# Sliding-window attention and two feed-forward nets on one core: the place of the softmax reciprocals up to step 9, and the first loads

## The chip, the core and the metric

The kernel runs on 1 core of one Trainium2 chip. The metric is the device time of one launch in microseconds (us), the median of three runs. Five engines work side by side, each through its own queue in order: TensorE (PE; its weight loads are listed as PEld), VectorE (DVE), ScalarE (ACT), GpSimd (POOL) and SyncE (SP, which here only issues transfers). They wait for each other through semaphores.

## What is computed

```python
scores = scale * np.matmul(q, k.transpose(0, 1, 3, 2))
keep = (pos[None, :] < n_sink) | ((rel >= 0) & (rel < window))
scores = np.where(keep, scores, -1e9)
a = np.exp(scores - np.max(scores, axis=-1, keepdims=True))
a = a / (np.sum(a, axis=-1, keepdims=True) + 1e-09)
attn_out = np.matmul(a, v)

x = attn_out rearranged to (1536, 512)
x = ((x @ w_a) * (x @ w_b)) @ w_out
h = np.maximum(x @ w_in, 0.0)
out = (h * h) @ w_out2
```

Batch 2, 8 heads, 768 tokens, head dimension 64, 4 sink tokens and a window of 128. The first net is 512 to 1536 to 512, the second 512 to 2048 to 512. All inputs are float32; the sink count and the window come in as data.

## The kernel before

**Groups and steps.** The attention is cut into 24 groups: 2 batches, 6 blocks of 128 queries, and in each block two halves of 4 heads. Group g belongs to block g // 2. The main loop (`attention_fast`) runs steps g = 0, 1, 2, ...; in step g each stage works on the group g plus its lag. The order of the work on PE, DVE, ACT and POOL is written out by hand: a list of (stage, lag) pairs is walked in every step, and each engine gets its instructions in the order of that list (`manual_schedule`). SP's transfers are placed by the scheduler.

```python
ORDER = [
    ("exp0", -1), ("exp1", -1), ("fm", 0), ("pst", -2), ("rec", -1), ("st", -2), ("fu", 0), ("scores0", 0),
    ("x0", -3), ("scores1", 0), ("x1", -3), ("xs", -3), ("abs", 0), ("xh", -3), ("ptp", -2), ("th", -2), ("cast", -2), ("soft0", 0), ("soft1", 0), ("sp", -1),
    ("norm", -1), ("warm", 0), ("fill", 0), ("normA", -1), ("normP", -1), ("xl", -3), ("stt", -1),
    ("lo", -2), ("ts", 0), ("lu", -2), ("stt2", -1)]
AT_FIRST = [x for x in ORDER if x[0] not in ("rec", "warm")]
AT_FIRST.insert(AT_FIRST.index(("soft1", 0)) + 1, ("rec", -1))
AT_FIRST.insert(AT_FIRST.index(("ptp", -2)), ("warm", 0))
```

Steps below `EARLY` (4) use AT_FIRST, all later ones ORDER. The two differ in two places. In ORDER the reciprocals of group g-1 (`rec`) stand on DVE in front of the maxima of group g (`soft0`, `soft1`); in AT_FIRST they stand behind them. In ORDER the warm matmuls stand on PE behind the transposes `ptp`; in AT_FIRST in front of them.

**The stages of one group,** with the lines of the kernel before: `scores0` and `scores1` (L243, PE, into the two PSUM tiles sc); `soft0` and `soft1` (DVE: a predicated copy L259, then two fused add-and-maximum operations L262 each); `exp0` and `exp1` (L270, ACT, four exponentials with their sums); `rec` (L275 and L276, DVE, the reciprocals of the sums); `sp` (L305 to L307, POOL, the sink columns); `norm` (L283, DVE), `normA` (L290, ACT) and `normP` (L295, POOL), which scale the rows of different heads; `pst` (L337, PE, transposes the sink columns) and `st` (L343, ACT, copies them); `ptp` (L313, PE, transposes the probabilities) and `th` (L317, ACT, copies them); `lu` (L328 and L330, POOL, two triangular selections); `x0`/`x1` (L362, from step 10 on L376, PE, times the values) and `xs` (L392, PE, the sink part); `xh` (L400, ACT) and `xl` (L403, DVE), the high and low half of the result.

A buffer rule: `scores0` of group g+1 writes the PSUM tile that `soft0` of group g has read. `pst` of group g-2 stands on PE in front of `scores0` of group g, in both lists.

**Beside the attention.** From step 4 on single pieces of the weights are decoded and split: `abs` (L589) and `cast` (L605) on ACT, `ts`, `stt`, `stt2`, `lo` (L593, L594, L597, L600, L607) on DVE; the pieces begin in steps 4, 8, 10, 11, 12 and so on (`DECODE`). From the end of step 11 on PE gets 12 matmuls of the first net (L720) in each step, `fill`. Below step 10 PE has `warm` instead: matmuls on zeros (L414) whose result nobody reads, as many per step as the table `WARM` says, and 14 before step 0. From step 10 on (`WIDE`) the product with the values is cut in two, `x0` and `x1`, and `x1` waits for a one-element memset on POOL (`mark`, L382) that itself waits for `x0`.

**Sinks.** The sink rows of the values of each batch are split into a high and a low part by `sink_split`: one copy on ACT (L220) and one subtraction on POOL (L221), emitted at the end of the steps in `VS` = (3, 12), the first for batch 0, the second for batch 1.

**Loads.** `load_kq(n)` brings block n's keys (L195) and queries (L196), `load_v(n)` the values (L202), all from SP. The first block comes in two halves. The keys in device memory lie in pieces of 136 floats (128 keys and 8 sink keys), 544 bytes, four pieces to a partition, without a gap. ACT issues only the 2 KB of `raw` (L81) and then loads its function table, placed in front of a one-column exponential (L85).

Of the kernel before, what the change touches and what calls it, by code (L numbers as in the profile page):

```python
# [10 lines left out]
F32 = mybir.dt.float32  # L11
F32R = mybir.dt.float32r
I32 = mybir.dt.int32
U32 = mybir.dt.uint32
AF = mybir.ActivationFunctionType
# [4 lines left out]
P = 128  # L20
# [14 lines left out]
AT_FIRST = [x for x in ORDER if x[0] not in ("rec", "warm")]  # L35
AT_FIRST.insert(AT_FIRST.index(("soft1", 0)) + 1, ("rec", -1))
AT_FIRST.insert(AT_FIRST.index(("ptp", -2)), ("warm", 0))
EARLY = 4
DECODE = [4, 8, 10, 11, 12, 13, 14, 15, 18, 19, 20]
WIDE = 10  # L40
VS = (3, 12)
FLAG = 22
SPARED = range(10, 18)
PINNED = 3
WARM0 = 14
WARM = {0: 2, 1: 4, 2: 6, 3: 8, 4: 9, 5: 6, 6: 6, 7: 6, 8: 6, 9: 6}
NQ, NV, NEX, NTH, NLU, NSP = 3, 5, 3, 2, 2, 2
T = 512
SW = P + SK
HK = P // 2  # L50
PREV = HK + SK
BIG = 8.0e9
# [24 lines left out]
def setup(tc, cp, tp, span):  # L77
    nc = tc.nc
    c = Attn()
    raw = cp.tile([P, 4], I32, name="raw")  # L80
    nc.scalar.dma_start(raw, span.bitcast(I32))  # L81
    ident = tp.tile([P, P], F32, name="ident")
    make_identity(nc, ident)
    warm = tp.tile([P, 1], F32, name="warm")
    nc.scalar.activation(warm, ident[:, 0:1], AF.Exp)  # L85

    v = nc.vector
    d = tp.tile([P, P], F32, name="d")
    nc.gpsimd.iota(d, pattern=[[-1, P]], base=0, channel_multiplier=1, allow_small_or_imprecise_dtypes=True)
    c.col = tp.tile([P, P], F32, name="col")  # L90
    nc.gpsimd.iota(c.col, pattern=[[1, P]], base=0, channel_multiplier=0, allow_small_or_imprecise_dtypes=True)
    c.upf = tp.tile([P, P], F32, name="up")
    v.tensor_scalar(out=c.upf, in0=d, scalar1=0.0, scalar2=None, op0=ALU.is_lt)

    c.rel = tp.tile([P, P], F32, name="rel")
    v.scalar_tensor_tensor(out=c.rel, in0=c.upf, scalar=float(P), in1=d, op0=ALU.mult, op1=ALU.add)
    rel0 = c.spare = tp.tile([P, P], F32, name="rel0")
    v.scalar_tensor_tensor(out=rel0, in0=c.upf, scalar=BIG, in1=d, op0=ALU.mult, op1=ALU.add)
    lo = cp.tile([P, 2], F32, name="lo_f")
    hi = cp.tile([P, 2], F32, name="hi_f")  # L100
    v.tensor_copy(lo, raw.bitcast(U32)[:, 0:4:2])
    v.tensor_copy(hi, raw[:, 1:4:2])
    par = cp.tile([P, 2], F32, name="par")
    v.scalar_tensor_tensor(out=par, in0=hi, scalar=4294967296.0, in1=lo, op0=ALU.mult, op1=ALU.add)
    c.ns = par[:, 0:1]
    c.w = par[:, 1:2]


    m0 = cp.tile([P, P], F32, name="m0")
    m1 = cp.tile([P, SW], F32, name="m1")  # L110
    m2 = cp.tile([P, SW], F32, name="m2")
    c.m = [m0, m1, m2]
    c.sink = tp.tile([P, P], F32, name="sink")
    out_of(v, c.sink, c.col, c.ns)
    out_of(v, m0, rel0, c.w)
    v.tensor_tensor(out=m0, in0=m0, in1=c.sink, op=ALU.max)
    c.identr = cp.tile([P, P], F32R, name="identr")
    v.tensor_copy(c.identr, ident)
    c.ident = c.identr.bitcast(F32)
    return c  # L120


# [34 lines left out]
def attention_fast(tc, ctx, c, cp, tp, q, k, v, vs_in, xh, xl, beside):  # L157


    nc = tc.nc  # L160
# [26 lines left out]
    queries, vals = {}, {}  # L187

    def load_kq(n, part=slice(0, H // 2)):
        if n >= B * NB:  # L190
            return
        if n not in queries:
            queries[n] = p2.tile([P, H // 2, P], F32, name="queries", tag="queries", bufs=NQ)
        b, i = divmod(n, NB)
        nc.sync.dma_start(keys[:, part, i], k[b, i, :, part])  # L195
        nc.sync.dma_start(queries[n][:, part], q[b, i, :, part])  # L196

    def load_v(n):
        if n >= B * NB:
# [4 lines left out]
    with tc.high_priority(offset=1000):  # L204
        load_kq(0, slice(0, 2))
        load_kq(0, slice(2, 4))
    load_kq(1)
    load_v(0)


# [1002 lines left out]
def layout(inputs):  # L1213

    import numpy as np

    def pairs(a, n):

        B, H, S, D = a.shape
        a = a.reshape(B, H // 2, 2, S // n, n, D).transpose(0, 3, 2, 5, 1, 4)  # L1220
        return a.reshape(B, S // n, 2 * D, H // 2, n)

    def blocks(w, inner):

        if inner:
            K, FF = w.shape
            w = w.reshape(K // P, P, FF // P, P).transpose(2, 1, 0, 3)
        return np.ascontiguousarray(w.reshape(-1, P, 512)).view(np.int64)

    q, k, v = (np.asarray(inputs[n]) for n in "qkv")  # L1230
    B, H, S, D = v.shape
    out = {"q": pairs(q, P)}
    sinks = pairs(k[:, :, 0:SK], SK)
    out["k"] = np.concatenate([pairs(k, P), np.broadcast_to(sinks, (B, S // P, *sinks.shape[2:]))], axis=4)
    out["v"] = v.reshape(B, H, S // P, P, D).transpose(0, 2, 3, 1, 4)

    vs = np.zeros((3, 4, SK, B, H // 4, 2, 2, D), v.dtype)
    for j in range(4):
        vs[:, j, :, :, :, j // 2, j % 2] = v[:, j::4, 0:SK].transpose(2, 0, 1, 3)
    out["vs"] = vs.reshape(12 * SK, B, H // 2, 2 * D)  # L1240
    out["span"] = np.broadcast_to(np.stack([inputs["n_sink"], inputs["window"]]).astype(np.int64), (P, 2))
    for n in _INS[5:]:
        out[n] = blocks(np.asarray(inputs[n]), not n.endswith("out"))
    return out
# [16 lines left out]
```

## Time and profile before

| | |
|---|---|
| median of 3 runs | 623.58 us (623.38 to 623.77) |
| profiled execution | 624.48 us |
| its span, first to last instruction | 622.8 us |
| PE busy | 608.0 us (98%) |
| DVE busy | 480.4 us (77%) |
| ACT busy | 303.5 us (49%) |
| POOL busy | 64.8 us (10%) |
| mean granted clock of PE | 0.996 |

The profiled execution took 0.9 us more than the median; 1.7 us of it lie outside the span. The busy shares are averages over stages with different limits: the attention ends at about 110 us, and the change is in its first 60 us. In the rows below a timeline row is: start in us, duration in us, engine, line, operation, what is written from what, shapes, how many were merged, and in brackets the idle time in front of it and who ended it. A PE row with a weight load in front of it is pipelined, so PE rows may overlap.

### The profile page before, as it was taken

Reading aid. Unit: us, or ns where it says so; the run is one execution under the profiler, and the core shown is the slowest. Engines: PE = TensorE matmul, PEld = TensorE weight load, DVE = VectorE, ACT = ScalarE, POOL = GpSimd, SP = SyncE. Lnnn points to the kernel's source line nnn. Section 1 sums busy time; section 2 is a strip of 40 time slices with the busy share of each in tenths; the row PEclk is TensorE's granted clock in tenths of the full one; section 3 lists DMA queues with packets and bytes.
Section 4 is the critical chain, followed back from the end, with each engine's and each line's share of the span. In section 5 each row is a group of like instructions: output and inputs, shape, how many; then the busy total and the mean of one; then the engine's idle time right before and its main releaser. Section 6 shows DMA issues by size and latency. Waiting matters only on the chain.

```text
span 622.8 us, 9656 instructions
## 1 busy us (share of the span) xinstructions
PE 608.0 (98%) x3525; PEld 494.4 (79%) x3525; DVE 480.4 (77%) x1079; ACT 303.5 (49%) x688; POOL 64.8 (10%) x157
## 2 busy tenths in 40 slices
PE   7989999999999999999999999999999999999995
PEld 4667778888888888888888888888888888888884
DVE  6889989369999948858869999977796779834352
ACT  5888887434744434434443554564453445232220
POOL 5665355400000000000000000000000000000000
PEclk9999999999999999999999999999999999999998
DMA  8934423012123313212302013232022202000032
GB/s 260 280 115 148 154 69 103 3 34 73 62 103 115 122 34 102 68 34 68 101 35 101 2 34 102 67 132 82 27 100 67 74 29 68 0 1 0 2 115 94
DMA packets 22041, 49.55 MB, mean 80 GB/s; under 512 B 2080, under 2 KB 8736, under 8 KB 21984
## 3 DMA queue, kind: packets, MB, share of 16 engines
q1 hardware_dynamic: 21696, 48.70, 24.5%
q8 instruction: 30, 0.49, 0.3%
q14 instruction: 27, 0.22, 0.1%
q10 hardware_dynamic: 288, 0.13, 0.1%
HBM read 45.68 MB, written 3.15 MB: 78 GB/s over the span
## 4 chain that ended last, share of the span: by engine, by line


## 5 line engine op out<-in xcount | busy, mean ns | idle before, releaser
L720 PE MATMUL psa<-xh,wh 128*128 128x512 f32 x224 | 88.6, 396 | 0.1
L720 PE MATMUL psa<-xh,wl 128*128 128x512 f32 x224 | 87.4, 390 | 0.0
L720 PE MATMUL psa<-xl,wh 128*128 128x512 f32 x224 | 87.3, 390 | 0.0
L980 PE MATMUL acc<-wh,gh 128*128 128x512 f32 x192 | 74.7, 389 | 0.0
L980 PE MATMUL acc<-wh,gl 128*128 128x512 f32 x192 | 74.7, 389 | 0.0
L980 PE MATMUL acc<-wl,gh 128*128 128x512 f32 x192 | 74.7, 389 | 0.0
L607 DVE TENSOR_TENSOR wl<-wtmp,wh 128x512 fp32r<-128x512 f32 x68 | 48.5, 717 | 17.2 <-ACT wh L605 17.0
L605 ACT CAST wh<-wtmp 128x512 fp32r<-128x512 f32 x68 | 42.3, 622 | 36.8 <-PE acc L980 10.0
L73 ACT CAST gh<-ks 128x512 fp32r<-128x512 f32 x48 | 29.7, 622 | 52.5 <-PE acc L980 52.5
L589 ACT ACTIVATE wtmp<-wraw 128x512 f32<-128x512 f32 x68 | 45.5, 673 | 19.3 <-DVE wl L74 12.7
L980 PE MATMUL acc<-gh,wh 128*128 128x512 f32 x136 | 52.9, 389 | 0.0
L980 PE MATMUL acc<-gl,wh 128*128 128x512 f32 x136 | 52.9, 389 | 0.0
L980 PE MATMUL acc<-gh,wl 128*128 128x512 f32 x136 | 52.9, 389 | 0.0
L720 PEld LDWEIGHTS psa<-xh,wh 128*128 128x128 f32 x224 | 42.1, 188 | 8.9 <-DVE gs L737 0.6
L720 PEld LDWEIGHTS psa<-xh,wl 128*128 128x128 f32 x224 | 42.0, 188 | 8.9
L597 DVE SCALAR_TENSOR_TENSOR wtmp<-wraw,wtmp 128x512 int32<-128x512 int32 x68 | 48.6, 719 | 0.4
L720 PEld LDWEIGHTS psa<-xl,wh 128*128 128x128 f32 x224 | 42.1, 188 | 8.2
L600 DVE SCALAR_TENSOR_TENSOR wtmp<-wraw,wtmp 128x512 int32<-128x512 int32 x68 | 46.4, 687 | 0.7
L980 PEld LDWEIGHTS acc<-wl,gh 128*128 128x128 f32 x192 | 36.0, 188 | 7.5
L980 PEld LDWEIGHTS acc<-wh,gh 128*128 128x128 f32 x192 | 36.0, 188 | 7.4
L980 PEld LDWEIGHTS acc<-wh,gl 128*128 128x128 f32 x192 | 36.0, 188 | 7.4
L74 DVE TENSOR_TENSOR gl<-ks,gh 128x512 fp32r<-128x512 f32 x48 | 32.8, 688 | 10.5 <-ACT gh L73 10.1
(177 smaller groups left out, 1279.5 us busy)
## 6 DMA issues: line engine op xcount, KB each, us to landing
wraw<-in_moe_w_out_dram SPq DMA_DIRECT2D x28, 512.0 KB, 3.5
wraw<-in_moe_w_in_dram SPq DMA_DIRECT2D x16, 512.0 KB, 3.5
wraw<-in_moe_w_a_dram SPq DMA_DIRECT2D x12, 512.0 KB, 3.5
wraw<-in_moe_w_b_dram SPq DMA_DIRECT2D x12, 512.0 KB, 3.4
values<-in_v_dram SPq DMA_DIRECT2D x12, 256.0 KB, 4.3
keys<-in_k_dram SPq DMA_DIRECT2D x11, 272.0 KB, 5.1
queries<-in_q_dram SPq DMA_DIRECT2D x11, 256.0 KB, 4.2
out_dram<-part SPq DMA_DIRECT2D x11, 256.0 KB, 2.2
```

Source lines behind the costliest of these rows:

```text
L73: nc.scalar.copy(hi, src)
L74: return (lo_eng or nc.vector).tensor_sub(lo, src, hi.bitcast(F32))
L589: a = nc.scalar.activation(tf, up.bitcast(F32), AF.Abs)
L597: nc.vector.scalar_tensor_tensor(out=t, in0=up, scalar=0x3FFFFFFF, in1=t, op0=ALU.bitwise_or, op1=ALU.bitwise_and)
L600: nc.vector.scalar_tensor_tensor(out=t, in0=low, scalar=29, in1=t, op0=ALU.logical_shift_right, op1=ALU.bitwise_or)
L605: nc.scalar.copy(hi, tf)
L607: nc.vector.tensor_sub(lo, tf, hi.bitcast(F32))
L720: self.tc.nc.tensor.matmul(ps, lhsT=w[:, kt, :], rhs=x[:, kt, ts], start=n == 0, stop=n == 3 * KT - 1)
L980: nc.tensor.matmul(acc["ps"][d], lhsT=a, rhs=b, start=n == 0, stop=n == acc["total"] - 1)
```

## The change

It has five parts. (1) `EARLY` goes from 4 to 10, so steps 4 to 9 walk AT_FIRST instead of ORDER. (2) The second sink split moves from the end of step 12 to the end of step 9. (3) The counts of warm matmuls change: 56 instead of 59 in all; 6 instead of 4 in step 1, 8 instead of 6 in step 2, 6 instead of 8 in step 3, 6 instead of 9 in step 4, 4 instead of 6 in step 7. (4) The keys lie in device memory with a pitch of 192 floats, 768 bytes, and 544 of them are read. (5) The queries of blocks 0 and 1 are issued by ACT instead of SP, block 1 is loaded at high priority, and the function table is loaded behind these issues.

```diff
-EARLY = 4
+EARLY = 10
-VS = (3, 12)
+VS = (3, 9)
-WARM = {0: 2, 1: 4, 2: 6, 3: 8, 4: 9, 5: 6, 6: 6, 7: 6, 8: 6, 9: 6}
+WARM = {0: 2, 1: 6, 2: 8, 3: 6, 4: 6, 5: 6, 6: 6, 7: 4, 8: 6, 9: 6}
+KP = 192
...
-    nc.scalar.dma_start(raw, span.bitcast(I32))
+    with tc.high_priority(offset=2000):
+        nc.scalar.dma_start(raw, span.bitcast(I32))
     ident = tp.tile([P, P], F32, name="ident")
     make_identity(nc, ident)
-    warm = tp.tile([P, 1], F32, name="warm")
-    nc.scalar.activation(warm, ident[:, 0:1], AF.Exp)
...
+    c.warm = tp.tile([P, 1], F32, name="warm")
...
-        nc.sync.dma_start(keys[:, part, i], k[b, i, :, part])
-        nc.sync.dma_start(queries[n][:, part], q[b, i, :, part])
+        nc.sync.dma_start(keys[:, part, i], k[b, i, :, part, 0:SW])
+        (nc.scalar if n < 2 else nc.sync).dma_start(queries[n][:, part], q[b, i, :, part])
...
     with tc.high_priority(offset=1000):
         load_kq(0, slice(0, 2))
         load_kq(0, slice(2, 4))
-    load_kq(1)
+        load_kq(1)
+        nc.scalar.activation(c.warm, c.ident[:, 0:1], AF.Exp)
     load_v(0)
...
+    out["k"] = np.pad(out["k"], ((0, 0),) * 4 + ((0, KP - SW),))
```

Where the instructions move is shown at three places. All lines of the changed kernel are one to three higher than those of the kernel before.

The first place is ACT's queue at the start of the program, up to the exponentials of groups 0 and 1 (`x2` and `x8` stand for two and eight like instructions). Before:

```order
L81 DMA raw<-in_span_dram 128x4
L85 ACT_TABLE_LOAD
L85 ACTIVATE warm<-ident 128x1
L270 ACTIVATE ex,ss<-ex,nb 128x128 x8
L317 COPY th<-ptp 128x512
```

And now:

```order
L83 DMA raw<-in_span_dram 128x4
L197 DMA queries<-in_q_dram 128x256 x2
L197 DMA queries<-in_q_dram 128x512
L209 ACT_TABLE_LOAD
L209 ACTIVATE warm<-identr 128x1
L272 ACTIVATE ex,ss<-ex,nb 128x128 x8
L319 COPY th<-ptp 128x512
```

Three issues of queries have come in front of the table load. SP loses the same three: its first issues are now the three of the keys of blocks 0 and 1, and then values of block 0.

The second place is DVE's queue in step 4, from the reciprocals or maxima with which it begins (`ss` holds the sums, `sc_169` and `sc_170` are the two PSUM tiles of the scores, `ISA` is the fused add-and-maximum and then the read of its result). Before:

```order
L275 TENSOR_SCALAR ss<-ss 128x4
L276 RECIPROCAL ss<-ss 128x4
L259 COPY_PREDICATED sc_169<-pick,sc_169 128x2x128
L262 ISA ex,nb<-sc_169,m_127 128x136
L262 ISA nb 128x1
L262 ISA ex,nb<-sc_169,m_127 128x136
L262 ISA nb 128x1
L259 COPY_PREDICATED sc_170<-pick,sc_170 128x2x128
L262 ISA ex,nb<-sc_170,m_127 128x136
L262 ISA nb 128x1
L262 ISA ex,nb<-sc_170,m_127 128x136
L262 ISA nb 128x1
```

And now:

```order
L261 COPY_PREDICATED sc_169<-pick,sc_169 128x2x128
L264 ISA ex,nb<-sc_169,m_125 128x136
L264 ISA nb 128x1
L264 ISA ex,nb<-sc_169,m_125 128x136
L264 ISA nb 128x1
L261 COPY_PREDICATED sc_170<-pick,sc_170 128x2x128
L264 ISA ex,nb<-sc_170,m_125 128x136
L264 ISA nb 128x1
L264 ISA ex,nb<-sc_170,m_125 128x136
L264 ISA nb 128x1
L277 TENSOR_SCALAR ss<-ss 128x4
L278 RECIPROCAL ss<-ss 128x4
```

The two instructions of the reciprocals of group 3 went from the front of the maxima of group 4 to behind them; it is the same in steps 5 to 9. In step 10 the reciprocals of group 9 stand in front of the maxima of group 10, as before.

The third place is ACT's queue in step 9, from the exponentials of group 8 to those of group 9. Before:

```order
L270 ACTIVATE ex,ss<-ex,nb 128x136 x4
L343 CAST st<-pst 96x128
L400 CAST xh<-x 128x2x128
L317 COPY th<-ptp 128x512
L290 ACTIVATE ex<-ex,ss 128x128
L270 ACTIVATE ex,ss<-ex,nb 128x136 x4
```

And now:

```order
L272 ACTIVATE ex,ss<-ex,nb 128x136 x4
L345 CAST st<-pst 96x128
L402 CAST xh<-x 128x2x128
L319 COPY th<-ptp 128x512
L292 ACTIVATE ex<-ex,ss 128x128
L222 CAST vs<-vsr 96x512
L272 ACTIVATE ex,ss<-ex,nb 128x136 x4
```

The copy of the second sink split stands between the scaling of group 8 and the exponentials of group 9. Its subtraction stands on POOL behind the selections of group 7 and in front of the mark of step 10.

## Rows read from the trace of the kernel before

**Rows 1.** Windows: stretch, then busy us of PE, PEld, DVE, ACT, POOL; PE clock; DMA.

```profile
6.00:8.00 2.00, 0.64 (x8) 0.31 (x4) 1.02 (x10) 2.00 (x12) 1.00 (x3) 1.00 1.00 311
...
80.00:90.00 10.00, 10.00 (x133) 7.97 (x132) 8.40 (x37) 7.86 (x29) 5.61 (x15) 1.00 0.23 73
```

**Rows 2.** Timeline, DVE: the first copy of the maxima of groups 3, 4 and 10.

```profile
11.17 0.41 DVE L259 COPY_PREDICATED sc<-pick,sc 128x256 f32<-128x256 int32 x1
...
16.95 0.41 DVE L259 COPY_PREDICATED sc<-pick,sc 128x256 f32<-128x256 int32 x1
...
41.12 0.41 DVE L259 COPY_PREDICATED sc<-pick,sc 128x256 f32<-128x256 int32 x1
```

**Rows 3.** Timeline, 0 to 9 us: first issue, queries of block 1, table load, group 2.

```profile
0.80 0.42 ACTq L81 DMA_DIRECT2D raw<-in_span_dram  x1
...
1.26 1.28 ACT L85 ACT_TABLE_LOAD   x1 [1.26 <-PEq L1201]
...
3.49 0.61 SPq L196 DMA_DIRECT2D queries<-in_q_dram  x1
...
4.99 0.40 ACT L270 ACTIVATE ex<-ex,nb 128x128 f32<-128x128 f32 x1 [2.24 <-DVE nb L262]
...
8.25 0.94 PE L243 MATMUL sc<-keys,queries 64*64 64x200 f32 x16 [1.61 <-DMA queries<-in_q_dram]
...
8.96 0.43 DVE L259 COPY_PREDICATED sc<-pick,sc 128x256 f32<-128x256 int32 x1 [1.90 <-PE sc L243]
```

**Rows 4.** Transfers within 4 to 5 us, and within 12 to 14 us.

```profile
DMA packets 267, 0.18 MB, mean 181 GB/s; under 512 B 25, under 2 KB 267, under 8 KB 267
...
DMA packets 362, 0.79 MB, mean 395 GB/s; under 512 B 36, under 2 KB 71, under 8 KB 362
```

**Rows 5.** Timeline, 13 to 17 us: from step 3 into step 4.

```profile
13.07 0.17 DVE L275 TENSOR_SCALAR ss<-ss 128x4 f32<-128x4 f32 x1
...
13.59 0.27 POOL L305 TENSOR_TENSOR ex<-ex,ss 128x32 f32<-128x32 f32 x1 [1.15 <-DVE ss L276]
...
14.44 0.61 ACT L220 CAST vs<-vsr 96x512 fp32r<-96x512 f32 x1
...
14.56 0.26 PE L337 MATMUL pst<-identr,sp 128*96 128x128 f32 x1 [0.94 <-POOL sp L307]
...
14.75 0.93 PE L243 MATMUL sc<-keys,queries 64*64 64x200 f32 x16
14.95 0.41 ACT L270 ACTIVATE ex<-ex,nb 128x136 f32<-128x136 f32 x1
...
16.65 0.17 DVE L275 TENSOR_SCALAR ss<-ss 128x4 f32<-128x4 f32 x1 [2.55 <-ACT ex L270]
```

**Rows 6.** Timeline, 35 to 39 us: PE's step 9 and what ACT does behind it.

```profile
35.73 1.09 PE L362 MATMUL x<-lu,values 128*64 128x128 f32 x16 [0.31 <-issue]
...
37.03 0.62 PE L313 MATMUL ptp<-identr,ex 128*128 128x128 f32 x4
...
37.39 0.65 PEld L414 LDWEIGHTS <-zero 128*128 128x128 bf16 x6
...
37.75 0.59 ACT L317 COPY th<-ptp 128x512 f32<-128x512 f32 x1
...
38.53 0.40 ACT L270 ACTIVATE ex<-ex,nb 128x136 f32<-128x136 f32 x1
```

**Rows 7.** Timeline, 26 to 28 us: the split of a decoded weight piece in step 6.

```profile
26.24 0.62 ACT L605 CAST wh<-wtmp 128x512 fp32r<-128x512 f32 x1
...
27.78 0.80 DVE L607 TENSOR_TENSOR wl<-wtmp,wh 128x512 fp32r<-128x512 f32 x1
```

**Rows 8.** Timeline: the net's first matmul; the second sink split and PE's step 13.

```profile
46.09 0.48 PE L720 MATMUL psa<-xh,wh 128*128 128x512 f32 x1
...
54.39 1.32 POOL L221 TENSOR_TENSOR vs<-vsr,vs 32x512 fp32r<-32x512 f32 x1
...
56.08 0.56 PE L376 MATMUL x<-lu,values 64*64 64x128 f32 x16 [0.84 <-POOL mark L382]
```

## Prediction, before the changed kernel was run

> **What bounds the kernel now.** I read the windows first, to see which engine is full where. From the first matmuls of the net on, PE has no gap: 10.00 of 10 us at 80 to 90 us, at full granted clock, while DVE has 8.40 [rows 1]. What is left there is a fixed amount of PE work, so a piece of time won or lost ahead of it moves the end by the same piece. Ahead of it PE waits: in 6 to 8 us it is busy for 0.64 of 2.00 us [rows 1]. There a step is as long as a chain across the engines, and the timeline shows which. I measure a step by the time T(g) at which DVE begins the maxima of group g: T(3) = 11.17, T(4) = 16.95, T(10) = 41.12 us [rows 2]. Steps 3 to 10 take 29.95 us together, of which the first takes 5.78 and the next six 24.17, 4.03 each. I read the timeline of the steps on both sides of the border at step 4, since there the kernel before already shows both orders and the passage between them.
>
> **Part 1, the order in steps 4 to 9.** What the move takes away is a wait: in the kernel before the reciprocals of group 3 stand in front of the maxima of group 4 and hold them until the exponentials of group 3 are done, 2.55 us of idle DVE [rows 5]. What it puts in its place is a longer chain. With the reciprocals behind the maxima, the sinks of group g-1 are scaled later on POOL, and their transpose (pst) stands on PE in front of the scores of group g+1. Nothing in the change moves that. So one step is at least: maxima of group g, then reciprocals, 13.07 - 11.17 = 1.90 [rows 2, 5]; to POOL's first operation 13.59 - 13.07 = 0.52; to pst 14.56 - 13.59 = 0.97, with PE idle for 0.94 just for this; to the scores of the group after next 14.75 - 14.56 = 0.19 [rows 5]; from scores to the first copy of the maxima 8.96 - 8.25 = 0.71 [rows 3]. The sum is **4.29 us** a step. It is no bound on ORDER, where the reciprocals come 1.9 us earlier in the step.
>
> Six steps of it, from T(3) to T(9), are 25.74 us. Two things come on top.
>
> In step 6 DVE subtracts the high half of a weight piece (lo), which waits for ACT's cast, which stands behind th. How late is th now? In the new order PE runs scores, values and sinks, six warm matmuls, then ptp, then ACT copies: 0.93 for the scores [rows 5], 37.03 - 35.73 = 1.30 for values and sinks, 0.65 for the warm ones that now stand in front, and 37.75 - 37.03 = 0.72 from ptp to th [rows 6]. That is 3.60 behind the scores, 2.89 behind T. Then 0.59 for th [rows 6], 0.62 for the cast and 0.80 for lo [rows 7] reach 4.90, and the maxima of group 7 are behind lo: 0.6 more than 4.29. In the kernel before DVE lagged PE by more, and the cast was done long before lo. It cannot cost under 0, and at most 0.6 more if th slips once more.
>
> At step 10 the order goes back: reciprocals of group 9, then the maxima of group 10. They wait for the exponentials of group 9, which on ACT stand behind th (2.89 after T(9)), the scaling, 38.53 - 37.75 = 0.78 from th to the exponentials [rows 6], and part 2's copy, 14.95 - 14.44 = 0.51; from the exponentials to the reciprocals 16.65 - 14.95 = 1.70 [rows 5], and 0.30 more to the maxima [rows 2, 5]. T(10) is then 6.18 after T(9). So the passage that cost 5.78 at step 4 is not gone; it is paid six steps later. The sum from T(3) to T(10) is 25.74 + 0.6 + 6.18 = 32.52 against 29.95: **2.6 us lost.**
>
> **Part 2, the second sink split.** In step 12 its subtraction keeps POOL for 1.32 us, the mark of step 13 waits behind it, and PE, by then the bound, idles for 0.84 [rows 8]. That goes: **0.84 won**. At the end of step 9 the copy's 0.51 is already in the 6.18. The 1.32 on POOL now stand in front of the mark of step 10. PE is not full there, but sinks, ptp and th of step 10 come later, and the first matmuls of the net hang on these. The wait there is between 0 (hidden under the wait of DVE) and the same 0.84; I take **0.5 lost**, nearer to the row, since ACT has its exponentials to finish at the same time and hides a part.
>
> **Part 3, the warm matmuls.** The two more in step 2 cost 0.2 (0.65 for six [rows 6]); the others are in the chains above, or in front of a wait that is longer. The granted clock is the risk: it was 1.00 even in the stretch with 0.64 us of PE in 2 [rows 1], and no stretch here will be emptier, so I cost it at nothing.
>
> **Parts 4 and 5, the start.** Before, the scores of group 2 begin at 8.25 and PE has waited 1.61 us for the queries of block 1 [rows 3]. They were issued at 3.49, sixth on SP, and 8.25 - 3.49 = 4.76 later the matmul runs. Now they are fourth on ACT. ACT's first issue is at 0.80 and takes 0.42; two halves follow, which I put at 0.45 each, between this 0.42 and the 0.61 of a whole one [rows 3]. So the issue comes at about 2.15, 1.3 us sooner, and the keys of block 1 move up on SP by two issues. If the 4.76 stays, scores begin at about 6.9. The bounds: nothing won, if the bytes and not the issues are the limit; and 1.5, where the exponentials and reciprocals of groups 0 and 1 hold the maxima of group 2 anyway. What speaks for the middle is that the transfers ran at 181 GB/s in 4 to 5 us and at 395 in 12 to 14 [rows 4], so the engines were not full when block 1 was under way. I take **1.3 won**. ACT's table load (1.28 us) moves behind the issues and ends at about 4.1, before the exponentials at 4.99 [rows 3]: nothing, and 0.8 lost if each issue took twice as long. The pitch of 768 bytes moves no more bytes; no row shows such packets, and I put it at nothing, with 0.2 either way.
>
> The Trainium skill has a rule that speaks against part 5: DMA: Bandwidth & Descriptors, section Issuing engines are not separate DMA queues, says that transfers started from several engines run on the same 16 DMA engines, and that only the sequencer's time to start them is saved, usually small beside the transfer. By that rule alone the start would win close to nothing. The 181 GB/s above is a row against it, but not a decisive one, as these were the small packets of keys.
>
> **The sum.** + 2.6 + 0.5 - 0.84 - 1.3 = + 0.96, rounded to + 1.0 us. The profiled execution of 624.48 would become 625.5; the median of the runs lies 0.9 lower, so the forecast is 623.58 + 1.0 = **624.6 us**. A measurement of this kernel tells about 0.2% from no change, 1.25 us: under 622.33 is faster, over 624.83 is slower. The point lies just inside no change; its own range, from 0.5 less to 0.8 more, crosses the border.
>
> **The rivals.**
> - *The bytes are the limit at the start.* Block 1 lands no sooner, since values of block 0 and keys of block 2 now follow on SP at once and share the engines. For it: 311 GB/s in 6 to 8 us, with the DMA share at 1.00 [rows 1]. Against it: rows 4. The 1.3 is gone: 624.6 + 1.3 = 625.9, slower. It decides if group 2's scores begin after 7.6 us, with half of the 1.3 gone. This is the Trainium skill's rule as a mechanism of this kernel.
> - *POOL's chain slips.* th, the two selections, values, sinks, ptp and th again make a loop as well. Before, it fitted into steps of 4.03 with the warm matmuls outside it; their 0.65 now stand inside, so it takes up to 4.68, which is 0.39 over the 4.29. If it is that long, six times 0.39 is 2.3, of which step 6 already has about 0.5: 1.8 more, 626.4, slower. It decides if steps 4, 5, 7 and 8 are longer than about 4.5 us.
> - *The passage at step 10 costs no more than another step.* If ACT ran so far ahead that the exponentials of group 9 were done when DVE comes to their reciprocals, T(10) would be about 4.3 after T(9), not 6.18, and the 0.5 of part 2 would be hidden: 624.6 - 1.9 - 0.5 = 622.2, faster. Against it: th of step 9 hangs on the scores of step 9 on PE, and those on the chain of 4.29.
> - *A step of the new order is no longer than one of the old.* That is the change not doing what the chain says: 4.03 instead of 4.29, six times 0.26, 623.0, no change.
>
> **How the numbers follow.** The forecast has 0.48, of which 0.30 within 0.2% and 0.18 above; the bytes at the start 0.17, slower; POOL's chain 0.15, slower; the passage 0.12, split 0.10 faster and 0.02 the same; the shorter step 0.08, the same. Together: faster 0.10, same 0.40, slower 0.50. The forecast is the likeliest single case, though the slower cases together weigh a little more. The range of 8 in 10 goes from 622.9, the shorter step, to 626.8, a little above the slip of POOL's chain; it leaves out the faster passage and the sum of two mishaps.
>
> **What the changed profile would show.** The scores of group 2 near 6.9 us; T(4) near 14.2 instead of 16.95; then copies of maxima some 4.3 apart, PE waiting for POOL in front of each pst; a gap of about 4.9 from T(6) to T(7) with lo in front; 6.2 from T(9) to T(10) with DVE idle for ACT; T(10) near 42.4 and the first matmul of the net near 47.9 instead of 46.09 [rows 8]; no wait for the mark in step 13. I am wrong if the steps are apart by 4.0 or less, if DVE does not idle in front of the reciprocals of group 9, or if the first matmul of the net comes before 46 us.

## The result, and the profile after

The changed kernel takes **631.65 us** (median of 4 runs, 631.14 to 631.92) against 623.67 us for the kernel before on the same chip (623.38 to 624.22): a ratio of 1.0122, 95% interval 1.011 to 1.0134. That is 8.0 us slower, where I had forecast 1.0 us slower, and outside my range. The profiled execution took 631.14 us, with a span of 629.3 us and a mean granted clock of 0.994. That is the shortest of the four; the other three had mean clocks of 0.989 to 0.991, so by this mean the profile shows the mildest case of what the clock did.

I read it as I had read the kernel before. First the start: the timeline from the first issues to the maxima of group 2.

```profile
1.27 1.42 ACTq L197 DMA_DIRECT2D queries<-in_q_dram  x3
2.72 1.28 ACT L209 ACT_TABLE_LOAD   x1 [2.72 <-issue]
...
5.26 0.40 ACT L272 ACTIVATE ex<-ex,nb 128x128 f32<-128x128 f32 x1 [1.04 <-DVE nb L264]
...
8.02 0.93 PE L245 MATMUL sc<-keys,queries 64*64 64x200 f32 x16 [0.36 <-DMA queries<-in_q_dram]
...
8.73 0.43 DVE L261 COPY_PREDICATED sc<-pick,sc 128x256 f32<-128x256 int32 x1 [0.97 <-PE sc L245]
```

The three issues on ACT take 1.42 us together, as costed, so block 1 is under way some 1.3 us sooner (worked out from its place as the last of the three); but the scores begin at 8.02, only 0.23 sooner than in [rows 3]. The transfers issued from 2 to 3 us show why, with block 1's queries in the second row (KB each, us from issue to landing):

```profile
keys<-in_k_dram SPq DMA_DIRECT2D x1, 272.0 KB, 6.0
queries<-in_q_dram ACTq DMA_DIRECT2D x1, 256.0 KB, 5.7
values<-in_v_dram SPq DMA_DIRECT2D x1, 256.0 KB, 6.0
```

The same queries in the kernel before, among the transfers issued from 3 to 4 us:

```profile
queries<-in_q_dram SPq DMA_DIRECT2D x1, 256.0 KB, 4.6
```

They landed 4.6 us after their issue, now 5.7: the earlier issue went together with a longer flight.

Then the steps. These are DVE's first copies of the maxima of groups 4 to 7, in the timeline, with the subtraction lo (L609) between the last two:

```profile
15.20 0.43 DVE L261 COPY_PREDICATED sc<-pick,sc 128x256 f32<-128x256 int32 x1 [1.29 <-PE sc L245]
...
19.50 0.43 DVE L261 COPY_PREDICATED sc<-pick,sc 128x256 f32<-128x256 int32 x1 [0.54 <-PE sc L245]
...
24.93 0.43 DVE L261 COPY_PREDICATED sc<-pick,sc 128x256 f32<-128x256 int32 x1 [0.24 <-PE sc L245]
...
29.64 0.70 DVE L609 TENSOR_TENSOR wl<-wtmp,wh 128x512 fp32r<-128x512 f32 x1 [1.48 <-ACT wh L607]
30.26 0.41 DVE L261 COPY_PREDICATED sc<-pick,sc 128x256 f32<-128x256 int32 x1
```

T(3) is 10.96, so the steps to T(9) = 38.78 are 4.24, 4.30, 5.43, 5.33, 4.23 and 4.29 us. Four of six are the forecast 4.29. The links of the forecast chain can be followed in the step from 15.20 to 19.50: reciprocals, POOL's first operation, pst, scores.

```profile
17.12 0.17 DVE L277 TENSOR_SCALAR ss<-ss 128x4 f32<-128x4 f32 x1
...
17.67 0.25 POOL L307 TENSOR_TENSOR ex<-ex,ss 128x32 f32<-128x32 f32 x1 [1.45 <-DVE ss L278]
...
18.66 0.27 PE L339 MATMUL pst<-identr,sp 128*96 128x128 f32 x1 [1.37 <-POOL sp L309]
...
18.86 0.93 PE L245 MATMUL sc<-keys,queries 64*64 64x200 f32 x16
```

They come 1.92, 0.55, 0.99 and 0.20 us one after another, and the next maxima 0.64 later; the forecast had 1.90, 0.52, 0.97, 0.19 and 0.71. One of the other two steps is long by lo, as forecast, and one is long by something I had excluded. The windows show it (columns as in [rows 1]).

```profile
10.00:20.00 10.00, 7.23 (x90) 4.66 (x88) 7.50 (x38) 8.94 (x35) 5.82 (x12) 1.00 1.08 358
...
20.00:21.00 1.00, 0.92 (x12) 0.75 (x14) 0.89 (x6) 0.00 (x0) 0.61 (x2) 0.74 1.10 360
21.00:22.00 1.00, 1.00 (x10) 0.67 (x6) 0.93 (x7) 0.00 (x0) 0.03 (x1) 0.50 1.14 295
...
40.00:50.00 10.00, 6.63 (x90) 4.28 (x88) 7.47 (x27) 6.82 (x25) 7.56 (x14) 1.00 0.43 133
...
51.00:52.00 1.00, 1.00 (x20) 0.88 (x18) 0.82 (x6) 0.53 (x1) 0.49 (x3) 0.60 0.06 16
52.00:53.00 1.00, 1.00 (x7) 1.00 (x6) 0.97 (x6) 0.37 (x1) 0.81 (x2) 0.50 0.79 172
```

Twice the granted clock falls to 0.50, that is from 2.4 to 1.2 GHz: from about 20.5 to 23.9 us and from about 51.2 to 54.6 us (worked out from the means of the windows at the edges). Both falls come behind stretches in which PE waited much: 7.23 and 6.63 of 10 us busy. In the same windows of the kernel before it was busy for 8.41 and 8.70, and its profiled execution shows no fall from 4 us on until PE's work is done:

```profile
10.00:20.00 10.00, 8.41 (x100) 5.31 (x99) 6.92 (x38) 8.76 (x35) 6.14 (x12) 1.00 1.07 353
...
40.00:50.00 10.00, 8.70 (x140) 6.45 (x130) 9.47 (x36) 8.95 (x33) 5.35 (x15) 1.00 0.53 163
```

The second fall covers the first matmuls of the net.

Last the passage at step 10, in the timeline: the last split, the mark, and DVE's return to reciprocals in front of the maxima.

```profile
42.19 0.58 ACT L319 COPY th<-ptp 128x512 f32<-128x512 f32 x1 [0.80 <-PE ptp L315]
...
42.97 0.60 ACT L222 CAST vs<-vsr 96x512 fp32r<-96x512 f32 x1
43.48 0.41 ACT L272 ACTIVATE ex<-ex,nb 128x136 f32<-128x136 f32 x1
...
44.89 1.26 POOL L223 TENSOR_TENSOR vs<-vsr,vs 32x512 fp32r<-32x512 f32 x1
...
45.19 0.99 DVE L277 TENSOR_SCALAR ss<-ss 128x4 f32<-128x4 f32 x1 [2.02 <-ACT ex L272]
46.21 0.18 DVE L278 RECIPROCAL ss<-ss 128x4 f32<-128x4 f32 x1
46.31 0.41 DVE L261 COPY_PREDICATED sc<-pick,sc 128x256 f32<-128x256 int32 x1
...
52.90 0.78 PE L722 MATMUL psa<-xh,wh 128*128 128x512 f32 x1
```

T(10) is 46.31 (41.12 before), and the first matmul of the net starts at 52.90 (46.09 in [rows 8]): 6.8 us late, which is all of the 6.66 us between the two profiled executions. The wait for the mark in step 13 is gone.

### The profile page after: what moved, and what is told of

The parts are those of the page before. It is cut to its first block, busy times and chain, and to the rows that moved or that the text cites. A ratio compares the mean times of both kernels' runs of the same rounds, so it can differ in the third digit from the quotient of the medians.

```text
span 629.3 us, 9650 instructions
## 1 busy us (share of the span) xinstructions
PE 611.9 (97%) x3522; PEld 497.4 (79%) x3522; DVE 480.1 (76%) x1079; ACT 303.5 (48%) x688; POOL 67.5 (11%) x157
## 4 chain that ended last, share of the span: by engine, by line
## 5 line engine op out<-in xcount | busy, mean ns | idle before, releaser
L609 DVE TENSOR_TENSOR wl<-wtmp,wh 128x512 fp32r<-128x512 f32 x68 | 48.0, 710 | 19.0 <-ACT wh L607 18.7
```

What stands on the lines that cost most here:

```text
L609: nc.vector.tensor_sub(lo, tf, hi.bitcast(F32))
```

## The experiments

My theory A: the new order is a longer chain (maxima, reciprocals, POOL's sp, pst, scores), and its waits let the granted clock fall, which costs more. Rivals: B, the changed table of warm matmuls lets the clock fall; C, the split in step 9 is the main cost; D, the falls of the clock lie beside other work and cost nothing.

The times T and the first net matmul ("net") are read off each timeline as above; "time" is the median, with its ratio to the kernel before on the same chip, whose own median lay between 623.13 and 623.80 us. T and net come from one profiled execution each; in order_back, split_back, turn_late and both_best that was the longest of the runs, so there the median and not the profile says what a change is worth.

| run | T(3) | T(6) | T(9) | T(10) | net | time | ratio (95%) |
|---|---|---|---|---|---|---|---|
| before | 11.17 | 25.15 | 36.76 | 41.12 | 46.09 | 623.67 | |
| after | 10.96 | 24.93 | 38.78 | 46.31 | 52.90 | 631.65 | 1.011 to 1.0134 |
| order_back | 10.99 | 24.73 | 36.24 | 41.54 | 47.46 | 623.53 | 0.9992 to 1.0012 |
| split_back | 11.25 | 24.63 | 38.57 | 44.74 | 52.31 | 628.88 | 1.0071 to 1.0105 |
| order_alone | 10.36 | 23.54 | 37.47 | 43.66 | 51.93 | 629.77 | 1.0093 to 1.0136 |
| start_alone | 11.39 | 25.35 | 36.86 | 41.22 | 46.18 | 623.66 | 0.9997 to 1.0016 |
| split_7 | 10.39 | 24.34 | 36.35 | 40.70 | 45.67 | 623.27 | 0.9978 to 1.0002 |
| no_zeros | 11.43 | 25.03 | 36.20 | 40.55 | 45.51 | 623.39 | 0.9979 to 1.0007 |
| both_best | 11.35 | 25.82 | 39.10 | 43.45 | 50.98 | 625.58 | 1.0005 to 1.0035 |
| order_to_7 | 10.79 | 24.71 | 39.23 | 44.53 | 51.60 | 628.57 | 1.007 to 1.0104 |
| turn_late | 10.69 | 23.63 | 37.00 | 44.59 | 52.67 | 629.67 | 1.0071 to 1.0114 |
| zeros_beside | 10.76 | 23.95 | 37.89 | 45.41 | 51.24 | 628.41 | 1.0064 to 1.0098 |
| zeros_split_7 | 11.01 | 24.21 | 38.32 | 44.50 | 50.96 | 628.16 | 1.0052 to 1.0093 |
| zeros_cast | 10.99 | 24.20 | 37.12 | 44.65 | 50.48 | 627.43 | 1.0039 to 1.008 |
| zeros_turn | 11.20 | 23.98 | 37.04 | 44.62 | 50.45 | 627.41 | 1.0037 to 1.0079 |
| zeros_all | 10.85 | 23.64 | 36.73 | 42.96 | 49.41 | 626.76 | 1.0033 to 1.0071 |

### Which part of the change

**order_back**, the changed kernel with the old border.

```
-EARLY = 10
+EARLY = 4
```

> The changed kernel with EARLY back at 4, the other parts kept. Theory A (the new order lengthens every step, and its longer waits let the granted clock of PE fall twice): nearly all of the 8 us comes back; first matmul of the net at 45.5 to 46.5 us, clock 1.00 throughout the first 60 us, 622.5 to 624.5. Theory B (the clock falls because fewer and otherwise placed warm matmuls stand there, whatever the order): the clock still falls at least once, 625 to 628. Theory C (the second split at step 9 is the cost): at least 2 us stay, 626 or more.

The whole 8 us come back: with the old order the other parts together are worth nothing either way. Theory A had expected a clock of 1.00 throughout; in the profiled execution it fell once, from 43.6 to 47 us, and the net began at 47.46. That fall is what B had asked for, but the time is A's.

**split_back**, the changed kernel with the split back in step 12.

```
-VS = (3, 9)
+VS = (3, 12)
```

> The changed kernel with the second sink split back at the end of step 12. A: the passage from the maxima of group 9 to those of group 10 shrinks from 7.53 us by 0.5 (ACT's copy) and 0.8 (DVE's add of 1e-9 no longer drawn out beside POOL's subtraction), and the wait for the mark of 0.84 in step 13 is back: 630 to 631.5. C: most of the loss goes, 627 or less.

The passage from T(9) to T(10) is 6.17 instead of 7.53. The time is 2.4 us less against the kernel before, more than A had expected and not as much as C needs; 5.6 us remain, so C falls as the main cause. The profile has one fall of the clock, from 49.7 to 53.1 us, instead of two, and T(5) to T(6) is 4.67 instead of 5.43; how much of the 2.4 us is the split's is asked in zeros_split_7. Between 10 and 20 us PE waits here as much as in the changed kernel, and no fall follows:

```profile
10.00:20.00 10.00, 7.26 (x93) 4.96 (x90) 7.48 (x40) 8.29 (x32) 5.53 (x11) 1.00 1.04 353
20.00:24.00 4.00, 3.21 (x39) 2.23 (x32) 3.70 (x16) 1.72 (x8) 2.50 (x6) 1.00 1.01 288
```

So the busy share of such a stretch does not decide alone whether a fall comes.

**order_alone**, the kernel before with the new border and nothing else.

```
-EARLY = 4
+EARLY = 10
```

> The kernel before with EARLY = 10 and nothing else, so with 59 warm matmuls in the old counts and the split in step 12. A: the steps 4 to 9 are 4.3 us or longer, the passage at step 10 some 6.5, first matmul of the net after 49 us, the clock falls at least once: 628 to 632. B (the counts are to blame): clock 1.00, at most 2.5 us slower than before, 626 or less. C: 626 or less, since the split stays in step 12.

With the old table of warm matmuls 6.5 of the 8.0 us are there, an interval that overlaps with that of the changed kernel, and the windows show a longer fall, from 44.5 to 51.4 us:

```profile
44.00:48.00 4.00, 3.18 (x39) 2.28 (x35) 2.29 (x13) 1.77 (x6) 2.06 (x7) 0.57 0.38 130
48.00:52.00 4.00, 3.98 (x55) 3.15 (x47) 3.70 (x15) 2.60 (x12) 2.38 (x6) 0.58 0.12 18
```

B falls.

**start_alone**, the kernel before with the queries on ACT and the pitch of 768 bytes (parts 4 and 5).

```
+KP = 192
...
+        (nc.scalar if n < 2 else nc.sync).dma_start(queries[n][:, part], q[b, i, :, part])
```

> The kernel before with the start alone: queries of blocks 0 and 1 issued by ACT, block 1 at high priority, table load behind, pitch of 768 bytes. If the bytes limit the landing of block 1 (what the trace of the changed kernel shows with scores of group 2 at 8.02 us): maxima of group 3 at 10.9 to 11.2, 623.3 to 624.0, no change. If the issues limit it, as the prediction took it: 622.0 to 622.8.

No change. Over all runs T(2) is between 8.06 and 8.97 with the old start and between 8.46 and 9.18 with the new one, so the spread of the landings is larger than what the start moves.

**split_7**, the kernel before with the split in step 7.

```
-VS = (3, 12)
+VS = (3, 7)
```

> The kernel before with the second sink split at the end of step 7. The wait of PE for the mark in step 13 (0.84 us) goes and nothing is behind the mark in step 10; ACT's copy of 0.51 stands in a step in which DVE is the bound. A: 622.4 to 623.0, a little faster. If ACT's copy is on the path there: 623.0 to 623.6.

PE's wait for the mark is gone and PE's timeline shows no wait over 0.15 us from the net's first matmul to 90 us; the median gains 0.4 us, less than can be told from nothing.

### Does the clock cost anything?

**more_zeros** and **order_zeros** add six to eight zero matmuls a step, and a few in front of x1, to the changed kernel and to order_alone, written into unused columns of the scores' tile.

```
+MORE = {3: 6, 4: 6, 5: 6, 6: 6, 7: 6, 8: 6, 9: 8, 10: 8}
...
+            nc.tensor.matmul(scs[0][:, 0, 272:512], lhsT=beside.zero, rhs=beside.zero[:, 0:1].to_broadcast([P, 240]),
...
+                more(MORE.get(g, 0) if name == "ptp" else 0)
```

> The changed kernel with matmuls on zeros added where PE only waits: 6 behind ptp in steps 3 to 8, 8 in steps 9 and 10, 6 and 4 in front of x1 in steps 10 and 11; they fill unused columns of a score tile and nobody reads them. Theory A (a part of the loss is the longer chain, a part the granted clock that falls because PE waits so much): clock 1.00 in the first 60 us; maxima of group 6 come 4.3 to 4.5 us behind those of group 5, not 5.43; first matmul of the net 48.5 to 50.5 instead of 52.90; 627.5 to 629.5. Rival D (the clock falls are an effect of the late steps and cost nothing, as PE waits there anyway): 631 to 632, whether or not the clock falls.

> The kernel before with EARLY = 10 alone and the same added zeros. A: the chain stays, maxima of group 10 at 43.3 to 44.0 us; the clock no longer falls at 45 to 51 us, so the first matmul of the net comes some 5 us behind the maxima of group 10, at 48.3 to 49.3 instead of 51.93: 625.5 to 627.0. D: 629 to 630.

Both missed their question: 668.98 and 667.14 us (ratios 1.0679 to 1.0739 and 1.0656 to 1.0708). A row of DVE in more_zeros:

```profile
32.80 0.43 DVE L263 COPY_PREDICATED sc<-pick,sc 128x256 f32<-128x256 int32 x1 [6.72 <-PE sc L423]
```

The maxima waited for my zeros (L423), which stood behind ptp: the two use different columns, so the wait was for the whole tile. The step became 10.5 us. They show how dear a wait is that closes a loop through all engines, and nothing on the clock.

**zeros_beside**, the same idea in tiles that nobody waits for at that moment, in PE's gaps alone.

```
+MORE = {3: 10, 4: 10, 9: 6}
+MORE_X = {10: 4, 11: 4}
...
+                if name == "ptp" and g in MORE:
+                    more(idle[0], MORE[g])
...
+            more(whole[:, 0, 2 * P:4 * P], MORE_X.get(now[0], 0))
```

> The changed kernel with zero matmuls added where TensorE stands idle, in tiles that no other engine waits for at that moment: 10 behind the transposes of the probabilities in steps 3 and 4, 6 there in step 9 (into the tile of the same step's zero matmuls), and 4 in front of the first half of the values in steps 10 and 11 (into unused columns of the tile x). The result stays the same. At about 0.11 us each they should fill the gaps of 1.4 to 1.8 us in front of L339 and 0.6 us in front of L378. Theory A (a longer chain, and on top of it the two falls of the granted clock, at 20.3 to 23.5 and 51 to 54.7 us, that come behind stretches in which TensorE waited): with TensorE kept busier the clock stays at 1.00 there; the step from the maxima of group 5 to those of group 6 goes from 5.43 to 4.3 to 4.5 us, the way from the maxima of group 10 to the first net matmul from 6.6 to about 5.5; time 629 to 630.5. Theory D (the falls of the clock lie beside other work and cost nothing): clock kept or not, the time stays at 631.1 to 631.9. If the clock falls all the same, nothing is decided.

628.41 us: 3.2 us come back by added work. The windows to set beside those of after:

```profile
10.00:20.00 10.00, 9.37 (x110) 6.53 (x110) 7.45 (x38) 8.94 (x35) 6.03 (x12) 1.00 1.07 364
...
20.00:22.00 2.00, 2.00 (x24) 1.59 (x25) 1.88 (x13) 0.37 (x1) 0.65 (x2) 1.00 1.12 302
...
52.00:54.00 2.00, 2.00 (x10) 1.62 (x9) 2.00 (x5) 2.00 (x10) 1.67 (x2) 1.00 1.05 308
```

PE is busy for 9.37 us in 10 to 20, the clock stays at 1.00, the step from T(5) to T(6) is 4.66 instead of 5.43, T(10) to net is 5.83 instead of 6.59, and behind the first net matmul the profiled execution lasts 577.2 us instead of 578.2, which I put down to the part of the second fall that lay in the full stage. D falls. The four steps without a fall take the same with and without the added zeros, 17.05 and 17.06 us, so these change nothing but the clock there; T(3) differs by 0.2 us, by the landing at the start. So about 3 of the 8.0 us are the clock's, and 4.8 are not.

**no_zeros**, the kernel before without the table's warm matmuls, and **both_best**, that together with the split in step 7.

```
+WARM = {}
```

> The kernel before without the 59 warm matmuls of steps 0 to 9 (the 14 ahead of step 0 stay). A: PE waits as long as in the changed kernel, the clock falls one to three times in the first 60 us, 1 to 2 us lost by each fall where PE is the bound: 625 to 629. D: the clock may fall but the chain does not run through the warm matmuls: 623 to 624.

> The kernel before with the split of the third part of the sinks' values in step 7 (the wait at the mark in step 13 was gone there) and without any of the zero matmuls of the table WARM. Each alone made no difference that could be measured (ratios 0.999 and 0.9993). Together: 622.5 to 623.4, ratio 0.998 to 1.0; a ratio above 1.001 would mean that the zero matmuls are needed where the order of step 7 changes.

Without the zeros the clock fell in the profile of no_zeros only from about 8.8 to 12.3 us, and the time did not change. In both_best, by nothing but another place for the split, it fell five times in the profiled execution, the longest of ten:

```profile
8.00:12.00 4.00, 4.00 (x42) 2.48 (x37) 2.59 (x14) 1.95 (x8) 1.23 (x2) 0.58 1.09 324
15.00:19.00 4.00, 4.00 (x42) 2.73 (x45) 2.52 (x14) 2.71 (x11) 2.83 (x6) 0.60 1.08 377
28.00:32.00 4.00, 4.00 (x35) 3.11 (x37) 3.76 (x17) 1.58 (x9) 2.00 (x6) 0.57 0.78 250
42.00:46.00 4.00, 3.68 (x46) 3.00 (x46) 3.71 (x16) 1.62 (x6) 1.39 (x5) 0.57 0.40 120
49.00:53.00 4.00, 4.00 (x30) 3.52 (x29) 3.79 (x15) 2.40 (x8) 2.21 (x6) 0.58 0.73 193
```

Its ten runs spread from 623.59 to 628.46 us, where split_7, with the zeros, spread from 622.43 to 624.49. My expectation for the sum of two harmless edits was wrong: the zeros are worth nothing in the order they were tuned for, and about 2 us in the one disturbed order that was tried.

### Where the rest goes

**order_to_7**, the changed kernel with the new order up to step 6 only (EARLY = 7).

> The changed kernel with the new order only up to step 6 (EARLY = 7 in place of 10). If the loss grows with each step that has the new order: steps 4 to 6 lose 0.3 each, step 6 another 1.0 by the wait of lo, and the passage from the new order to the old (6.2 us instead of 4 to 5 without a split beside it) is paid once wherever it lies: 623.6 + 0.9 + 0.6 to 1.0 + 1.3 = 626.2 to 627. If the passage and the clock behind it make up nearly all, it stays above 629; if only the late steps matter, it is at 623.5 to 624.5.

628.57 us, more than expected: the passage now lies between T(6) and T(7), takes 6.88 us, and the clock falls all the same, from about 20.2 to 23.6 and from 44.1 to 51 us. So the loss does not grow step by step: three steps of the new order already cost 5.0 of the 8.0 us, with the passage back and two falls of the clock among it.

**turn_late**, the changed kernel with pst and st behind the second half of the scores, and **zeros_turn**, the same on zeros_beside.

```
+AT_FIRST = [x for x in AT_FIRST if x[0] not in ("pst", "st")]
+AT_FIRST[AT_FIRST.index(("scores1", 0)) + 1:AT_FIRST.index(("scores1", 0)) + 1] = [("pst", -2), ("st", -2)]
```

> The changed kernel, with the transpose of the sinks' probabilities (pst) and its copy (st) moved behind the second half of the scores in the early steps' order, so that the scores no longer queue on TensorE behind the transpose that waits for POOL's sp. Theory A (step = maxima, sp on POOL, pst, scores, maxima): the steps of 4.2 to 4.3 us become 3.6 to 4.0, bounded next by TensorE's own row or by DVE; first net matmul 1.5 to 3 us earlier than 52.9; time 628.5 to 630. If the steps stay at 4.2 to 4.3, the chain is another than the one I named, and the time stays at 631 to 632.

> zeros_beside with the transpose of the sinks' probabilities and its copy behind the second half of the scores (the edit of turn_late). Theory A: with the clock held, the steps from T(3) to T(9) take 25.3 us or less (27.1 in zeros_beside, 26.3 in turn_late with 3.5 us at half clock among them), the first net matmul is at 49.5 to 50.2, and the time is 626.7 to 627.7. If another loop (probabilities turned, copied, selected on POOL, values, sinks) is as long as the one taken away, T(3) to T(9) stays at 26 to 27 and the time at 628 to 628.7.

turn_late takes 629.67 us, 2.0 less than the changed kernel, as A had it. In its profile T(9) comes 1.8 us earlier, but the clock is at 0.50 for some 10 us from 45 us on and takes most of it: this execution, with a mean clock of 0.986, took 631.08 us, where the one with 0.997 took 628.26. With the clock held, zeros_turn wins 1.0 us: the six steps from T(3) take 25.84 us instead of 27.13, that is 1.3 of the 1.8 us or more that A had expected, and no longer alike, from 3.1 to 5.2 us. PE now waits for POOL's selections instead:

```profile
33.74 1.24 PE L368 MATMUL x<-lu,values 128*64 128x128 f32 x16 [0.89 <-POOL lu L334]
```

The next loop is nearly as long.

**zeros_cast**, zeros_beside with ACT's cast ahead of the copy th.

```
+AT_FIRST.remove(("cast", -2))
+AT_FIRST.insert(AT_FIRST.index(("th", -2)), ("cast", -2))
```

> zeros_beside with the cast of the weight pieces on ScalarE moved ahead of the copy th in the early steps' order. Theory L (the 5.42 us from T(6) to T(7), 1.1 over a step of 4.3, are the wait of lo for the cast behind th): that step becomes 4.3 to 4.5, DVE no longer waits 1.48 us for wh, and the first net matmul comes 0.6 to 1.1 us earlier; time 627.4 to 627.9. If the step stays above 5, the cast waits for something else, or th has become late behind the cast, and the time stays at 628.1 to 628.7.

As expected: T(6) to T(7) is 4.39 instead of 5.42, and 1.0 us comes back. In ACT's timeline the cast now stands in front of the wait for ptp, and th is no later than the transposes allow:

```profile
26.96 0.62 ACT L623 CAST wh<-wtmp 128x512 fp32r<-128x512 f32 x1
...
27.86 0.59 ACT L323 COPY th<-ptp 128x512 f32<-128x512 f32 x1 [0.28 <-PE ptp L319]
```

**zeros_split_7**, zeros_beside with VS = (3, 7).

> zeros_beside with the third split in step 7 in place of step 9. Theory P (the split beside the passage costs 0.5 to 1.3 us: its subtraction keeps POOL for 1.26 us ahead of the mark, slows DVE's addition to 0.99 us, and its copy stands in front of the exponentials): the passage from T(9) to T(10) goes from 7.5 to about 6.2 us as in split_back and order_alone, step 8 or 9 grows by at most 0.3, the wait at the mark in step 13 stays gone, and the time is 627.1 to 627.7. If the split costs the same 1 us wherever it lies in the new order (step 8 to 9 longer by 1), the time stays at 628.1 to 628.7.

The passage is 6.18 instead of 7.52, but the time gains only 0.25 us, a miss: DVE meets another wait in the next step,

```profile
47.78 0.70 DVE L623 TENSOR_TENSOR wl<-wtmp,wh 128x512 fp32r<-128x512 f32 x1 [0.76 <-ACT wh L621]
```

and T(10) to net grows from 5.83 to 6.46. The wait of lo stood behind the wait in the passage. So of the 1.3 us that the split costs in the passage, only 0.25 show in the time once the clock is held.

**zeros_all**, all three on zeros_beside.

> zeros_beside with the edits of zeros_split_7, zeros_cast and zeros_turn together. If the three are separate pieces of the path, their gains add: 628.41 - 0.25 - 0.98 - 1.00 = 626.2, between 625.8 and 626.6, with T(3) to T(9) at about 24.8 us and the passage to T(10) at about 6.2. If they are one piece seen three times (the next loop, POOL's selections and values, sets the step as soon as one goes), the time stays at 627.0 to 627.5. Either way it is above 623.6, since the passage back to the old order is still paid.

626.76 us, between the two answers: 1.65 of the 2.2 us add up. The steps from T(3) to T(9) did not: 25.88 us, no better than zeros_turn alone. What is left above the kernel before is some 3.6 us. By the profiles, which differ by 2.2 us, it is not in the steps: from T(3) to T(9) the kernel before, with its own passage among them, takes 25.59. The passage of 6.23 us against 4.36 and the way from T(10) to the net, 6.45 against 4.97 with the wait of lo in it, are 3.4 us longer, and 1.1 us come back behind, where the wait for the mark is gone. No run takes that passage away while it keeps the new order, so this share is read off and not shown by an experiment. No version with the new order came nearer to the kernel before than this; split_7 on the old order is the best seen, and not told apart from it.

## Why the prediction was wrong

The sum by its own terms, in the profiled executions (forecast 625.5, measured 631.14, so 5.6 us to explain):

| term | forecast | measured | missed by |
|---|---|---|---|
| T(3), the start (parts 4, 5) | 9.9 | 10.96 | 1.1 |
| the four steps to T(4), T(5), T(8), T(9) | 17.16 | 17.06 | -0.1 |
| T(5) to T(6) | 4.29 | 5.43, or 4.66 with the clock held | 0.8 clock, 0.4 rest |
| T(6) to T(7), with lo | 4.9 | 5.33 | 0.4 |
| passage, T(9) to T(10) | 6.18 | 7.53 | 0.5 th, 0.8 split |
| T(10) to the net's first matmul | 5.5 | 6.59, or 5.83 with the clock held | 0.8 clock, 0.3 rest |
| from there to the end | 577.5 | 578.2, or 577.2 with the clock held | 1.1 clock, -0.4 rest |

**The step that failed is part 3**: "The granted clock is the risk: it was 1.00 even in the stretch with 0.64 us of PE in 2 [...], and no stretch here will be emptier, so I cost it at nothing." It measured 2.6 us in the profiles (0.8 + 0.8 + 1.1) and 3.2 in the medians. One short empty stretch was a poor witness for a row of half-idle steps. I looked at the depth of one gap; what differed between the two kernels were the whole stretches in front of the falls, and even these do not settle it (split_back). The Trainium skill, in TensorE: Matmul & The Clock Gate, section HAM oscillation — how this bites in real kernels, warns of a near case: where each burst of matmuls is followed by a wait for a transfer that is longer than the burst, the clock goes down at every burst. The falls in the windows above agree in kind, but here the waits were for other engines and no longer than 1.4 us; I had not weighed that section.

The clock alone does not carry the time out of my range: with the clock held, zeros_beside is still at 628.41 us, above the 626.8. Two more terms were mis-sized, the start by 1.1 us and the passage by 1.35, and the range left out the sum of two mishaps. The 0.2 us that part 3 had for step 2 never entered the sum.

**Parts 4 and 5, the start: the rival was right.** I took 1.3 us won and measured 0.2, which is within the spread of T(2). The Trainium skill's rule that I had cited (DMA: Bandwidth & Descriptors, section Issuing engines are not separate DMA queues), that transfers of all issuing engines run on the same DMA engines, agrees with the trace: the flight of block 1's queries went from 4.6 to 5.7 us. My row against it was one microsecond of small packets. start_alone shows no gain from the start in the time.

**Part 1, the chain, was right in its size and as a cause in part.** Four steps of 4.23 to 4.30 for a forecast 4.29, link by link, and lo as the long one at step 6. zeros_cast shows the wait of lo (1.0 us; I had 0.6, since th came 3.58 behind T and not 2.89), zeros_turn that the transpose behind sp sets the step, though with POOL's selections close behind it. The passage was too short in the forecast: th came 3.41 behind T(9) and not 2.89. Without a split beside it the passage measured 6.17 to 6.23 us; that this is also my 6.18 is luck, since mine had the split's copy of 0.51 in it and would have been 5.67 without. POOL's chain as a rival in its own right, with the steps over 4.5, did not come: with the clock held only one of them is, by 0.16 us.

**Part 2, the split.** The 0.84 at the mark was won: the wait is gone, and with the clock held the stretch from the net's first matmul on is 577.2 us, against 578.4 before (624.48 - 46.09). In the passage the split cost 1.36 us (7.53 against 6.17 in split_back). The copy's 0.51 of this was in the sum; the rest is DVE's addition, which took 0.99 us and not 0.17, where I had put 0.5 later on. zeros_split_7 shows that all but 0.25 of this hides a wait which comes next anyway.

The rivals of a cheaper passage and of a shorter step both failed. None of my cases held a fall of the clock, which is one reason why the range was too narrow on the slow side.

## What to carry to other kernels

A reordering that makes TensorE wait a little in every step can cost twice: once for the longer chain, and again when the granted clock falls behind it; so compare TensorE's busy share over whole stages of both orders, not only its emptiest stretch, and take a lower share as a risk of a fall and not as a forecast of one. Zero matmuls in the gaps gave 3.2 us back here, but only in tiles that no engine is waiting for. When a border between two orders is moved, its passage moves with it, and what stands beside the new place (a cast, a split) has to be costed there. Where one profiled execution shows a fall, the times and mean clocks of the others tell how typical it is.

## What the runs showed that I had not expected

- The granted clock fell to 0.50 for 3.4 us at a time (after) up to about 10 us (turn_late), with PE busy between waits and never idle for long: the longest wait in front of a PE row from 10 to 20 us of after is 1.37 us. The same zero matmuls made no difference in one order (no_zeros, 0.9979 to 1.0007) and about 2 us in its neighbour (both_best against split_7).
- DVE's addition of reciprocals, 128x4, took 0.99 us instead of 0.17 [rows 5] while POOL's subtraction of 1.26 us ran; both ended within 0.03 us of each other (45.19 + 0.99 and 44.89 + 1.26). The Trainium skill has this in SBUF — State Buffer, section Who interferes with whom: the two engines share one pair of ports, which some forms of DVE's instructions need, and whichever comes second then waits until the other's instruction ends. The two ends in the trace agree; without the split beside it (order_alone) the addition took 0.17 us.
- Some 1.3 us off the issue of a transfer at a busy start went with only 0.2 us off its landing.
